# Spectral-filter weights: −k rows loaded from GpSimd's queue beside the +k rows from SyncE's, rows of 513 elements in place of 514

## The chip, the cores and the metric

The kernel runs on one core of one Trainium2 chip. The metric is the device time of one execution in microseconds (us). Engines are named as the profile names them: PE (TensorE, matmuls), PEld (its weight loads), DVE (VectorE), ACT (ScalarE), POOL (GpSimd), SP (SyncE, which only issues DMAs here); "SPq" is the issuing queue of SP.

## What is computed

Two spectral filters of the same input, mixed by a gate (B = 1, S = 2048, D = 1024, all bfloat16):

```python
def _ref(x, w_r, w_i):                       # once with A's weights, once with B's
    X = rfft2(x.astype(float32), axes=(-2, -1))
    X = X * (w_r + 1j * w_i)                 # w_r, w_i: [2048, 513]
    return irfft2(X, s=(S, D), axes=(-2, -1)).astype(bfloat16)

g = sigmoid((x * gate_w).sum(-1, keepdims=True))
out = g * A + (1 - g) * B
```

## The kernel before, in words

The Fourier transforms are matrix products with constant tables. The work runs in this order:

- **First stage** (L386 to L405): for each pair of row groups, DVE folds x (`fold`, L366, four TENSOR_TENSOR), PE multiplies by the table `FM` (eight matmuls for a group), ACT copies the result from PSUM to SBUF (tile `R3`). Along the way a gate row is made and summed (`gate_row`, L380; the matmuls of L413, which read the keys `zrow`).
- **Middle loop** (L538 on), t from 0 to 20. A pass issues, in this order: `stage_d(t)` (eight matmuls against `DM`, the result copied into the ring buffer, "RING"), `stage_s2(t-1)` (six matmuls against `S2`, the result X copied into `R4`), `stage_i1(0, t-5)` (eight matmuls against `KI`, the result V of filter A copied into `R1`), and in every second pass `prod(b, m)` (four DVE TENSOR_TENSOR: the complex product of X and the weights). At the end of pass 0 it calls `wload(1)`, then loads the tables `DI` and `RM`. The three matmul groups of a pass share three PSUM slots in turn (`slot`, L287), so a slot is free again when the copy of the group three before it has been made.
- **Then** `stage_i1(1, t)` with `stage_dinv(0, t)` (inverse transform of A) and the gate mix, and at last `stage_dinv(1, t)`, the final mix and the stores.

`ev` (L296) picks ACT or DVE for a copy out of PSUM by adding up estimated costs; the change alters none of them. Each engine executes its instructions in the order in which the program adds them.

The **weights** lie in SBUF as 128 partitions of 32 rows of `NS` = 514 elements: tile `R5` for filter A (b = 0), tile `R2` for filter B (b = 1). Partition 8j + 4·pm + ii holds 16 frequencies: pm = 0 is the +k rows, pm = 1 the −k rows, read with a negative step. One DMA of `wload` (L340) fills 16 partitions, those of one (pm, ii) with j = 0 to 15, with 16 rows each, of the real (c = 0) or the imaginary (c = 1) part. Tile `R2` is used before that for the gate row; tile `R1` holds x first, and V of filter A later. The profile calls `R1` to `R5` all "R".

The **order of engines and queues** is made by a small scheduler from keys that each operation reads and writes (L137):

```python
for k in reads:
    o.deps |= self.writer[k]
...
for k in writes:
    o.deps |= self.writer.get(k, set())
    o.deps |= self.readers.get(k, set())
for k in reads:
    self.readers.setdefault(k, set()).add(o)
for k in writes:
    self.writer[k] = {o}
    self.readers[k] = set()
```

So an operation that writes a key waits for the key's last writer and for all that have read it since. The DMAs of one `dma(...)` call (L318) are one operation with one semaphore, and a wait for it (L199) is a wait until all of its DMAs have landed; the wait stands in the waiting engine's queue ahead of the instruction. `allx` (L418) is the list of the keys ("x", 0) to ("x", 15); the first copy of V of filter A, in `stage_i1(0, 0)`, writes all of them (L482), since V takes the place of x. `wload(1)` writes ("W", 1) and the keys "zrow" and "gwt" (L362), since it takes the place of the gate row.

Of the kernel before, what the change touches and what calls it, by code (L numbers as in the profile page):

```python
# [7 lines left out]
AP = bass.AP  # L8
BF = dt.bfloat16

NS = 514
# [223 lines left out]
def bass_gated_mix__spectral_gfnet__spectral_gfnet__prompt_kernel(  # L235
# [6 lines left out]
    def sb(name, n, dty=BF):  # L242
        t = nc.alloc_sbuf_tensor(name, [128, n], dty)
        pit[id(t)] = n
        return t

    def ap(t, off, dims, p0=0, np_=128):
        return AP(t, p0 * pit[id(t)] + off, [[pit[id(t)], np_]] + [list(d) for d in dims])
# [18 lines left out]
    X5 = sb("X5", 32)  # L267
# [19 lines left out]
    def slot():  # L287
        s = slot_n[0] % nslots[0]
        slot_n[0] += 1
        return s  # L290

    def dve(ns, fns, reads, writes):
        load["dve"] += ns
        return S.op("dve", fns, reads, writes)

    def ev(n, outap, inap, reads, writes, eng=None, bias=0.0):  # L296
        ca, cd = 170 + 0.833 * n, 150 + 1.04 * n
        if eng is None:
            eng = "act" if load["act"] + ca <= load["dve"] + cd + bias else "dve"
        load[eng] += ca if eng == "act" else cd  # L300
        if eng == "act":
            S.op("act", lambda e: e.activation(outap, inap, ACT.Copy), reads, writes)  # L302
        else:
            S.op("dve", lambda e: e.tensor_copy(outap, inap), reads, writes)  # L304

    def pslot(s, off, dims, p0=0, np_=128):
        return ap(PS, s * 1024 + off, dims, p0, np_)
# [4 lines left out]
    def mm(o, l, r, start, stop):  # L312
        return lambda e: e.matmul(o, l, r, start=start, stop=stop, skip_group_check=True)  # L313

    def tt(o, a, b, op):
        return lambda e: e.tensor_tensor(out=o, in0=a, in1=b, op=op)  # L316

    def dma(eng, pairs, reads, writes, kind=True):  # L318
        S.op(eng, [lambda e, d=d, s=s: e.dma_start(d, s) for d, s in pairs], reads, writes, dma=kind)  # L319
# [19 lines left out]

    def wload(b):  # L340

        prs = []
        T = WR[b]
        P = pit[id(T)]
        for ii in range(4):
            for c in range(2):
                for pm in range(2):
                    src = wsrc[b][c]
                    n = src.shape[-1]

                    def part(r0, step, k0, k1, m=n + 1):
                        prs.append((AP(T, (4 * pm + ii) * P + (2 * k0 + c) * NS, [[8 * P, 16], [2 * NS, k1 - k0], [1, m]]),
                                    AP(src.tensor, src.offset + r0 * n, [[128 * n, 16], [step * n, k1 - k0], [1, m]])))
                    if pm == 0:
                        part(16 * ii, 1, 0, 16)
                    elif ii < 3:
                        part(80 + 16 * ii, -1, 0, 16)
                    else:
                        part(127, -1, 1, 2, n)
                        part(126, -1, 2, 16)  # L360
                        part(64, 1, 0, 1)
        dma("sp", prs, [], [("W", b)] + (["zrow", "gwt"] if b else []))  # L362
    wload(0)


# [44 lines left out]
    for n2 in range(16):  # L410
        w = ap(R2, n2 * 128, [[1, 128]], 0, 1)
# [6 lines left out]
    allx = [("x", m) for m in range(16)]  # L418
# [34 lines left out]
    def prod(b, m):  # L453

        T = WR[b]
        x = ap(R4, 2 * m * 1024, [[1024, 2], [512, 2], [1, 512]])
        w = ap(T, 2 * m * 2 * NS, [[2 * NS, 2], [NS, 2], [1, 512]])
        ws = ap(T, 2 * m * 2 * NS + NS, [[2 * NS, 2], [-NS, 2], [1, 512]])
        r = [("X", 2 * m), ("X", 2 * m + 1), ("W", b)]
        p = PO + m % 2 * 2048  # L460
        dve(1230, tt(ap(RING, TO, [[1024, 2], [512, 2], [1, 512]]), x, w, ALU.mult), r, ["t0"])
        dve(1230, tt(ap(RING, TO + 2048, [[1024, 2], [512, 2], [1, 512]]), x, ws, ALU.mult), r, ["t1"])
        for c, op in enumerate((ALU.subtract, ALU.add)):
            t = TO + 2048 * c
            dve(680, tt(ap(RING, p + c * 512, [[1024, 2], [1, 512]]), ap(RING, t, [[1024, 2], [1, 512]]),
                        ap(RING, t + 512, [[1024, 2], [1, 512]]), op), [f"t{c}"], [("P", m % 2, c)])
# [3 lines left out]
    def stage_i1(b, kg):  # L470
        s = slot()
        p = PO + kg // 2 % 2 * 2048 + kg % 2 * 1024
        z = 512 if kg == 0 else 0
        fns = []
        for lb in range(4):
            for c in range(2):
                w = ap(RING, p + c * 512 + lb % 2 * 256 + lb // 2, [[2, 128]])
                fns.append(mm(pslot(s, lb * 256, [[1, 256]]), w, ap(KI, z + c * 256, [[1, 256]]), c == 0, c == 1))
        S.op("pe", fns, [("P", kg // 2 % 2, 0), ("P", kg // 2 % 2, 1), "KI"], [("ps", s)])
        w = [("V", b, kg)]  # L480
        if kg == 0:
            w += allx if b == 0 else [("W", 0)]  # L482
        ev(1024, ap(VR[b], kg * 8, [[128, 128], [1, 8]]), pslot(s, 0, [[8, 128], [1, 8]]), [("ps", s)], w)

    def x512():
# [2 lines left out]
    def p512(b):  # L488
        T, o = WR[b], b * 96
        x = ap(X5, 0, [[16, 2], [1, 16]])  # L490
        w = ap(T, 512, [[NS, 2], [2 * NS, 16]])
        ws = ap(T, NS + 512, [[-NS, 2], [2 * NS, 16]])
        r = ["X5", ("W", b)]
        dve(100, tt(ap(P5, o, [[16, 2], [1, 16]]), x, w, ALU.mult), r, [("p5", b, 0)])
        dve(100, tt(ap(P5, o + 32, [[16, 2], [1, 16]]), x, ws, ALU.mult), r, [("p5", b, 1)])
        for c, op in enumerate((ALU.subtract, ALU.add)):
            dve(100, tt(ap(P5, o + 64 + 16 * c, [[1, 16]]), ap(P5, o + 32 * c, [[1, 16]]),
                        ap(P5, o + 32 * c + 16, [[1, 16]]), op), [("p5", b, c)], [("P5", b, c)])
# [39 lines left out]
    for t in range(16 + 5):  # L538
        if t < 16:
            stage_d(t)  # L540
        if 1 <= t < 17:
            stage_s2(t - 1)
        if t >= 5:
            stage_i1(0, t - 5)
        if t >= 2 and t % 2 == 0:
            prod(t // 18, t // 2 - 1 - t // 18 * 8)
        if t == 0:
            wload(1)
            cload("sp", DI, "DI", 2048)
            cload("sp", RM, "RM", 2048)  # L550
        if t == 17:
            x512()
            p512(0)
            p512(1)
        if t == 19:
            v512(0)
            v512(1)
# [14 lines left out]
    for t in range(16 + LAG):  # L572
        if t < 16:
            stage_i1(1, t)
            if t % 2 == 1 and t // 2 + 2 < 8:
                prod(1, t // 2 + 2)
        if t in (8, 10, 12, 14):
            gmix((t - 8) // 2)
        if t == 15:
            v512_row(1)  # L580
        if t >= LAG:
            stage_dinv(0, t - LAG)
# [64 lines left out]
```

## Time and profile before

| | |
|---|---|
| median of 2 runs | 159.06 us (158.91 to 159.21) |
| the profiled execution, its own time | 158.91 us |
| its span in the profile | 157.1 us |
| busy time: PE / ACT / DVE / POOL | 125.9 / 121.8 / 120.4 / 0.2 us |
| loaded from HBM / stored | 15.18 / 4.19 MB |
| mean granted TensorE clock | 0.962 |

The span runs from the first to the last instruction of the program; 1.8 us of the execution's own time lie outside it. The page cuts the span into 40 slices of 3.93 us and gives in tenths how busy each engine was. A line such as "A <- B: 8.4, 5, 6.4" in the view of the waits says that A waited for B 8.4 us in total, five times, at most 6.4 us. In the timeline, each row has the start, the length, the engine, the line of the code, and out<-in; "x2" says that two instructions were merged into the row.

### The profile page before, as it was taken

Reading aid. Unit: us, or ns where it says so; the run is one execution under the profiler, and the core shown is the slowest. Engines: PE = TensorE matmul, PEld = TensorE weight load, DVE = VectorE, ACT = ScalarE, POOL = GpSimd, SP = SyncE. Lnnn points to the kernel's source line nnn. Section 1 sums busy time; section 2 is a strip of 40 time slices with the busy share of each in tenths; the row PEclk is TensorE's granted clock in tenths of the full one; section 3 lists DMA queues with packets and bytes.
Section 4 is the critical chain, followed back from the end, with each engine's and each line's share of the span. In section 5 each row is a group of like instructions: output and inputs, shape, how many; then the busy total and the mean of one; then the engine's idle time right before and its main releaser. Section 6 shows DMA issues by size and latency. Waiting matters only on the chain.

```text
span 157.1 us, 2545 instructions
## 1 busy us (share of the span) xinstructions
PE 125.9 (80%) x1015; PEld 90.5 (58%) x1024; DVE 120.4 (77%) x193; ACT 121.8 (78%) x132; POOL 0.2 (0%) x4
## 2 busy tenths in 40 slices
PE   0145887788989999999657999959999899898930
PEld 0144653445665777776434688947778576565600
DVE  0689999000589898989999999949923788989893
ACT  3045789719999899799934699999998599888860
POOL 0000000000000000000000000000000000000000
PEclk9999999999999999999975599999999999999997
DMA  5999999999999970000000000000000033243433
GB/s 147 321 417 425 288 232 229 238 220 215 220 224 223 225 259 0 0 4 0 0 0 0 1 4 0 0 0 4 0 0 1 4 121 146 86 183 112 160 129 140
DMA packets 13230, 19.55 MB, mean 124 GB/s; under 512 B 1569, under 2 KB 9889, under 8 KB 12834
## 3 DMA queue, kind: packets, MB, share of 16 engines
q1 hardware_dynamic: 13072, 19.39, 45.2%
q8 instruction: 8, 0.13, 0.4%
q14 instruction: 4, 0.03, 0.1%
q10 hardware_dynamic: 146, 0.00, 0.1%
HBM read 15.18 MB, written 4.19 MB: 123 GB/s over the span
## 4 chain that ended last, share of the span: by engine, by line
PE 37%; ACT 30%; DVE 21%; issue 6%; DMA 4%; SPq 1%; DVEq 0%
PE PS L313 37%; ACT RING L302 14%; ACT R L302 13%; DVE RING L316 11%; DVE R L316 6%; DMA R<-in_A_x_dram 4%; DVE RING L304 3%; ACT GROW L565 1%; ACT V L302 1%; SPq L319 1%; DVEq L213 0%
## 5 line engine op out<-in xcount | busy, mean ns | idle before, releaser
L302 ACT ACTIVATE R<-PS 128x1024 bf16<-128x1024 f32 (+1 forms) x80 | 76.0, 1038 | 19.1 <-PE PS L313 19.0
L316 DVE TENSOR_TENSOR RING<-R 128x2048 bf16<-128x2048 bf16 (+1 forms) x48 | 48.0, 1041 | 14.1 <-ACT R L302 8.4
L302 ACT ACTIVATE RING<-PS 128x1024 bf16<-128x1024 f32 x40 | 42.9, 1138 | 8.0 <-PE PS L313 6.8
L316 DVE TENSOR_TENSOR RING<-RING 128x512 bf16<-128x512 bf16 (+1 forms) x96 | 44.6, 509 | 2.7 <-ACT RING L302 1.4
L313 PE MATMUL PS<-KI,RING 128*128 128x256 bf16 x256 | 35.4, 289 | 4.3 <-DVE RING L316 2.2
L313 PE MATMUL PS<-DI,R 128*128 128x256 bf16 x256 | 32.7, 273 | 1.5 <-DVE RING L304 1.2
L313 PEld LDWEIGHTS PS<-KI,RING 128*128 128x128 bf16 x256 | 25.0, 103 | 11.2 <-ACT R L302 2.9
L313 PEld LDWEIGHTS PS<-DI,R 128*128 128x128 bf16 x256 | 24.4, 98 | 8.4 <-DVE RING L304 2.2
L313 PE MATMUL PS<-FM,R 128*128 128x128 bf16 x128 | 11.6, 263 | 13.3 <-DVE R L316 13.3
L313 PEld LDWEIGHTS PS<-FM,R 128*128 128x128 bf16 x128 | 9.9, 120 | 15.1 <-DVE R L316 14.7
L313 PE MATMUL PS<-RING,S 128*128 128x1 bf16 (+2 forms) x91 | 15.8, 304 | 1.3 <-ACT RING L302 1.1
L313 PE MATMUL PS<-DM,R 128*128 128x256 bf16 x128 | 16.5, 273 | 0.3 <-ACT RING L302 0.2
L313 PEld LDWEIGHTS PS<-DM,R 128*128 128x128 bf16 x128 | 11.8, 98 | 3.0 <-ACT RING L302 1.1
L313 PEld LDWEIGHTS PS<-RING,S 128*128 128x128 bf16 x96 | 7.8, 97 | 7.5 <-ACT RING L302 1.4
L304 DVE CAST RING<-PS 128x1024 bf16<-128x1024 f32 x8 | 10.0, 1250 | 1.7 <-PE PS L313 1.7
L316 DVE TENSOR_TENSOR R<-RING 128x1024 bf16<-128x1024 bf16 x16 | 10.4, 688 | 0.3
L313 PE MATMUL PS<-R,FM 128*128 128x512 bf16 x30 | 9.1, 379 | 1.3 <-DVE RING L304 1.3
L313 PE MATMUL PS<-RING,DM 128*128 128x512 bf16 x30 | 9.1, 379 | 0.1
L313 PE MATMUL PS<-R,G 128*1 128x512 bf16 x32 | 7.5, 378 | 0.7 <-ACT R L302 0.7
L304 DVE CAST R<-PS 128x1024 bf16<-128x1024 f32 x4 | 4.9, 1222 | 3.1 <-PE PS L313 3.1
L316 DVE TENSOR_TENSOR FM<-RM,GROW 128x512 bf16<-128x512 bf16 x4 | 1.7, 422 | 5.4 <-ACT GROW L565 5.4
L316 DVE TENSOR_TENSOR ZG<-PS,GS 128x16 bf16<-128x16 f32 x1 | 0.2, 175 | 6.8 <-PE PS L313 6.8
(25 smaller groups left out, 28.7 us busy)
## 6 DMA issues: line engine op xcount, KB each, us to landing
out_dram<-RING SPq DMA_DIRECT2D x16, 256.0 KB, 2.0
R<-in_A_x_dram SPq DMA_DIRECT2D x3, 1024.0 KB, 10.6
R<-in_A_w_r_dram SPq DMA_DIRECT2D x7, 257.0 KB, 10.4
R<-in_A_w_i_dram SPq DMA_DIRECT2D x7, 257.0 KB, 10.3
R<-in_B_w_r_dram SPq DMA_DIRECT2D x7, 257.0 KB, 7.1
R<-in_B_w_i_dram SPq DMA_DIRECT2D x7, 257.0 KB, 8.1
R<-in_A_x_dram SPq DMA_DIRECT2D x2, 512.0 KB, 5.2
FM<-c_F SPq DMA_DIRECT2D x1, 512.0 KB, 5.2
```

The source lines that it names most:

```text
L302: S.op("act", lambda e: e.activation(outap, inap, ACT.Copy), reads, writes)
L304: S.op("dve", lambda e: e.tensor_copy(outap, inap), reads, writes)
L313: return lambda e: e.matmul(o, l, r, start=start, stop=stop, skip_group_check=True)
L316: return lambda e: e.tensor_tensor(out=o, in0=a, in1=b, op=op)
L319: S.op(eng, [lambda e, d=d, s=s: e.dma_start(d, s) for d, s in pairs], reads, writes, dma=kind)
L565: S.op("act", lambda e: e.activation(ap(GROW, 0, [[1, 512]]), misc(7, 0, [[1, 512]]), ACT.Sigmoid), ["m7"], ["GROW"])
```

## The change

`wload` collects the DMAs of the two signs in two lists. The +k list goes out from SP as before; the −k list goes out from POOL, as an operation that also reads the key ("x", 15). The keys become ("W", b, 0) and ("W", b, 1), and both operations of `wload(1)` write "zrow" and "gwt". Each row is read as 513 elements; before, all but two DMAs of a call read 514 (the padding column of the tile took the extra one). With that, the two DMAs for the first 15 rows of the last −k block become one. A call makes 8 DMAs on SP and 10 on POOL; before it was 20 on SP. The readers of the weights wait for both keys.

```diff
     def wload(b):
 
-        prs = []
+        both = ([], [])
         T = WR[b]
         P = pit[id(T)]
...
                 for pm in range(2):
                     src = wsrc[b][c]
                     n = src.shape[-1]
-
-                    def part(r0, step, k0, k1, m=n + 1):
-                        prs.append((AP(T, (4 * pm + ii) * P + (2 * k0 + c) * NS, [[8 * P, 16], [2 * NS, k1 - k0], [1, m]]),
-                                    AP(src.tensor, src.offset + r0 * n, [[128 * n, 16], [step * n, k1 - k0], [1, m]])))
+                    prs = both[pm]
+
+                    def part(r0, step, k0, k1):
+                        prs.append((AP(T, (4 * pm + ii) * P + (2 * k0 + c) * NS, [[8 * P, 16], [2 * NS, k1 - k0], [1, n]]),
+                                    AP(src.tensor, src.offset + r0 * n, [[128 * n, 16], [step * n, k1 - k0], [1, n]])))
                     if pm == 0:
                         part(16 * ii, 1, 0, 16)
                     elif ii < 3:
                         part(80 + 16 * ii, -1, 0, 16)
                     else:
-                        part(127, -1, 1, 2, n)
-                        part(126, -1, 2, 16)
+                        part(127, -1, 1, 16)
                         part(64, 1, 0, 1)
-        dma("sp", prs, [], [("W", b)] + (["zrow", "gwt"] if b else []))
+        dma("sp", both[0], [], [("W", b, 0)] + (["zrow", "gwt"] if b else []))
+        dma("pool", both[1], [("x", 15)], [("W", b, 1)] + (["zrow", "gwt"] if b else []))
     wload(0)
...
-        r = [("X", 2 * m), ("X", 2 * m + 1), ("W", b)]
+        r = [("X", 2 * m), ("X", 2 * m + 1), ("W", b, 0), ("W", b, 1)]
...
         if kg == 0:
-            w += allx if b == 0 else [("W", 0)]
+            w += allx if b == 0 else [("W", 0, 0), ("W", 0, 1)]
...
-        r = ["X5", ("W", b)]
+        r = ["X5", ("W", b, 0), ("W", b, 1)]
```

## The prediction

> **What bounds the kernel now.** I read the 40 slices first, for the stretch in which weights move, then the waits, the timeline around the first use of filter A's weights, and the chain of work at that place.
>
> ```profile
> PE   0145887788989999999657999959999899898930
> DVE  0689999000589898989999999949923788989893
> ACT  3045789719999899799934699999998599888860
> PEclk9999999999999999999975599999999999999997
> DMA  5999999999999970000000000000000033243433
> GB/s 147 321 417 425 288 232 229 238 220 215 220 224 223 225 259 0 0 4 0 0 0 0 1 4 0 0 0 4 0 0 1 4 121 146 86 183 112 160 129 140
> ```
>
> The DMA engines are busy without a break for 15 slices (to 59 us). x and tables move at 417 to 425 GB/s, the weights at 215 to 238, half of that. But does anybody wait for them?
>
> ```profile
> DVE RING L316 <- ACT R L302: 8.4, 5, 6.4
> DVE RING L316 <- DMA R<-in_A_x_dram: 5.7, 2, 4.4
> SPq L319 <- PE PS L313: 4.4, 1, 4.4
> ```
>
> (The third line is from SP's own list of waits.) In the whole list, x is the only load that an engine waits for. The first product (DVE RING L316) waits 6.4 us for X, copied by ACT, and not for the weights. By the trace's landings filter A's last weight DMA lands at 37.6 us (issued 29.3, 8.3 later) and filter B's at 57.3; their first readers start at 40.9 and after 76. So faster weights have nothing to shorten: gain 0. Only a loss is possible, where a wait moves. The place that matters is the middle loop:
>
> ```profile
> 34.32 1.23 SPq L319 DMA_DIRECT2D R<-in_B_w_r_dram  x2
> ...
> 40.91 2.36 DVE L316 TENSOR_TENSOR RING<-R 128x2048 bf16<-128x2048 bf16 x2 [6.41 <-ACT R L302]
> ...
> 45.16 1.03 PE L313 MATMUL PS<-KI,RING 128*128 128x256 bf16 x8
> ...
> 46.05 2.00 ACT L302 ACTIVATE R<-PS 128x1024 bf16<-128x1024 f32 x2
> ...
> 47.20 1.06 PE L313 MATMUL PS<-RING,S 128*128 128x512 bf16 x6
> ...
> 47.84 1.42 ACT L302 ACTIVATE RING<-PS 128x1024 bf16<-128x1024 f32 x1
> ```
>
> 34.32 is when SP is released to load filter B's weights (the PE wait of 4.4 us above: the matmuls that read "zrow"). 45.16 is `stage_i1(0, 0)`; of the two ACT copies at 46.05 the second is its V. The chain has them too:
>
> ```profile
> 46.26 1.79 ACT R L302 x2
> 48.05 1.22 ACT RING L302
> 49.27 0.05 issue
> 49.32 3.71 PE PS L313 x30
> ```
>
> So V(0,0) holds ACT from about 47.15 to 48.05, on the path that sets the end; then comes the copy of `stage_d(6)`, and PE runs from there almost without a gap (11.89 us of the 12 from 60 to 72).
>
> [...] 232 GB/s from 18 to 34 us, 221 from 38 to 54. [...] SP's unhindered weight DMAs (34.3 to 40 us) take 0.61 us each, [...] no run here shows GpSimd's. [...] from 76.80 to 80.21 PE was busy 1.47 of 3.41 us, and from 80.21 to 90.45 the clock was 0.50[...].
>
> **The change part by part.**
>
> *Rows of 513.* 64 of the 8192 rows were 1026 bytes already; their packet records take 86 ns on average, those of 1028 bytes 79. They sit in one-row DMAs beside semaphore writes, so from 0 to +9% on a row. I take 0; +9% would add 0.9 us to the +k half of filter B.
>
> *Filter A's weights.* SP's eight DMAs follow the tables as before. POOL (busy 0.2 us in all) starts when the last x load lands, 15.7 us (issued 3.1, 12.6 later). [...] Cost 0, hidden by ACT's X chain. Without that cover, every us past 40.9 would delay the first product, and it is reached only if POOL needs over 24 us.
>
> *Extra semaphore waits* at DVE and ACT: the issue gaps in the chain are 0.02 to 0.06 us, so under 0.2 in all; taken as 0.
>
> *The key ("x", 15).* It is meant to start POOL late, but it also makes both POOL operations readers of x. `stage_i1(0, 0)` writes all keys of x, and `wload(1)` was added before it, in pass 0. So the copy V(0,0) now waits until filter B's −k weights have landed. Before, these had until 76 us. Behind that wait in ACT's queue stand the copy of `stage_d(6)` and all later ones; PE can still do `stage_d(6)` and `stage_s2(5)` (to 48.3), then it has no free slot. DVE can do one copy and two products ahead, which are not on the path.
>
> *The keys "zrow" and "gwt".* Both operations of `wload(1)` write them, so the second, POOL's, waits for the landing of the first, SP's. The halves of filter B come one after the other, not beside each other.
>
> When does V(0,0) start, then? SP released 34.3. Eight DMAs of 16 x 16 x 1026 B = 0.263 MB at 221 GB/s: 9.5 us. Issue and landing: a store of 256 KB lands after 2.0 us, of which 0.6 is data at 425 GB/s, so 1.4. +k landed: 34.3 + 1.4 + 9.5 = 45.2. [...] the last, small DMA lands 1.2 later (R<-V of 4 KB: 1.7 from issue, 0.57 of it issuing): 61.3. Stall: 61.3 - 47.15 = 14.2 us, and nothing hides it, since PE, DVE and ACT all run dry. DI and RM, behind SP's half, move meanwhile; needed past 90.
>
> *PE clock.* PE idles from 48.3 to about 62.3, [...] PE is the bound there, [...] I take 2.5 (0 if the clock isn't cut).
>
> Sum: 14.2 + 2.5 = 16.7. Profiled execution: span 157.1 to 173.8, its time 158.9 to 175.6; against the median of 159.06, 0.15 above it, 175.8, said as **176 us**.
>
> Both ends of POOL's price: if it writes as fast as SP issues (6.1 us for ten), the transfer binds: 45.2 + 1.4 + 9.5 = 56.1, stall 9.0, time 168 without and 170.6 with the slow clock. Above, 2.5 us for each DMA, four times SP's 0.61 (an estimate): 25 us, V at 71.4, stall 24.2, time 186.
>
> **Rivals.**
>
> 1. *The transfer binds* (writing takes under 11.5 us): 168 to 172. [...]
> 2. *POOL is slow* (over 19 us for ten DMAs): 180 to 187. For it: nothing in this trace bounds it from above.
> 3. *Not slower:* POOL's second operation is not held by SP's. It then starts at 34.3, [...] and with ten DMAs in less than 47.15 - 34.3 - 1.2 = 11.6 us V(0,0) is not late: 159. It decides at 1.16 us for each DMA. Against: the rule on writers in the scheduler; it needs my reading of the keys to be wrong.
> 4. *Faster,* [...] no engine waits for weights, so this has next to no room.
>
> **How the numbers follow.** Chances: forecast (172 to 180) 0.59, rival 1 0.17, rival 2 0.17, rival 3 0.05, rival 4 0.02. What can be told from no change is about 2% (3.2 us): slower 0.93, within 0.05, faster 0.02. The range 168 to 186 takes in the ends of rival 1 and most of rival 2, and leaves out rivals 3 and 4. The forecast's own range is 172 to 180.
>
> **What would show it.** In the profile after: ACT R L302 idle some 14 us before V(0,0), ended by a DMA issued by POOL; a hole in PE, DVE and ACT from about 48 to 61 us, and a clock of 0.5 in the slices just after it; POOL's first filter B DMA just after the +k half has landed (about 45); the later stages as long as before. Wrong, if POOL's filter B DMAs start near 34, if V(0,0) starts on time, or if the hole lies at 40.9 (filter A late).

## The result, and the profile after

The changed kernel takes 181.97 us (median of 2 runs, 180.98 to 182.96) against 159.06: a ratio of 1.144, interval 1.117 to 1.171. A later set with 6 runs (below) gave 1.144 again, 1.139 to 1.149. The forecast was 176, in a range of 168 to 186. The profiled execution took 182.96 us with a span of 181.1: 24.0 us more than before. It is the slower of the two runs.

The 40 slices of the page (now 4.53 us each) have the hole:

```profile
PE   0445998889600004999999559999699989998950
DVE  0799990008950000268998999998693469899994
ACT  2255498399400005689889844899999959987970
PEclk9999999999975555599999985999999999999997
DMA  6999999999998990000000000000000003334334
GB/s 180 331 423 374 171 224 222 218 165 166 166 243 169 161 144 0 0 5 2 0 0 4 0 0 0 5 0 0 4 0 0 1 4 116 116 138 157 121 114 171
```

Slices 12 to 15 are empty on PE and ACT (DVE still has one copy and two products in slices 11 and 12), the clock is cut from within the hole to the first slices after it, and the weights move at 144 to 169 GB/s where one queue works alone (slices 9 to 11 and 13 to 15). The view of the waits names the two waits of the forecast:

```profile
POOL R L319 <- DMA R<-in_B_w_i_dram: 32.5, 1, 32.5
ACT R L302 <- DMA R<-in_B_w_i_dram: 22.0, 1, 22.0
POOL R L319 <- DMA R<-in_A_x_dram: 15.4, 1, 15.4
DVE RING L316 <- DMA R<-in_A_w_i_dram: 6.8, 1, 6.8
```

POOL waits for filter B's +k half, ACT for its −k half. The last line is new as well: the first product now waits for filter A's weights, but they come only 0.4 us after X, which it waited for before (41.36 against 40.94, the end of X's copy); when the same kernel ran again (e9), they came in time. The timeline around the hole:

```profile
46.09 1.10 ACT L302 ACTIVATE R<-PS 128x1024 bf16<-128x1024 f32 x1
46.38 1.05 PE L313 MATMUL PS<-DM,R 128*128 128x256 bf16 x8
47.26 1.06 PE L313 MATMUL PS<-RING,S 128*128 128x512 bf16 x6
...
53.93 0.58 POOL L319 DMA_DIRECT2D R<-in_B_w_r_dram  x1 [32.47 <-DMA R<-in_B_w_i_dram]
...
69.20 1.02 ACT L302 ACTIVATE R<-PS 128x1024 bf16<-128x1024 f32 x1 [22.01 <-DMA R<-in_B_w_i_dram]
70.12 1.31 ACT L302 ACTIVATE RING<-PS 128x1024 bf16<-128x1024 f32 x1
...
70.28 1.89 PE L313 MATMUL PS<-KI,RING 128*128 128x256 bf16 x8 [21.96 <-ACT R L302]
```

69.20 is V(0,0). PE did `stage_d(6)` and `stage_s2(5)` and then stood still for 22 us; the first eight matmuls after the hole take 1.89 us where such a group took 1.03. The chain of work runs through the two halves one after the other:

```profile
38.94 14.71 DMA R<-in_B_w_i_dram
53.65 0.28 issue
53.93 4.41 POOL R L319 x8
58.34 0.57 POOLq L213
58.91 10.21 DMA R<-in_B_w_i_dram
69.11 0.02 issue
```

### The profile page after: what moved, and what is told of

It is laid out like the page before. It is cut to its first block, busy times and chain, and to the rows that moved or that the text cites. A ratio compares the mean times of both kernels' runs of the same rounds, so it can differ in the third digit from the quotient of the medians.

```text
span 181.1 us, 2542 instructions
## 1 busy us (share of the span) xinstructions
PE 129.4 (71%) x1015; PEld 91.9 (51%) x1024; DVE 120.6 (67%) x193; ACT 121.6 (67%) x132; POOL 11.3 (6%) x24
## 4 chain that ended last, share of the span: by engine, by line
ACT 31%; PE 27%; DMA 17%; DVE 13%; issue 5%; SPq 3%; POOL 2%; POOLq 0%; DVEq 0%; ACTq 0%
PE PS L313 27%; ACT R L302 20%; DMA R<-in_B_w_i_dram 14%; ACT RING L302 8%; DVE RING L316 7%; DMA R<-in_A_x_dram 4%; DVE R L316 3%; SPq L319 3%; DVE RING L304 3%; POOL R L319 2%; ACT GROW L566 1%; ACT L566 1%; ACT V L302 1%; POOLq L213 0%; DVEq L213 0%
## 5 line engine op out<-in xcount | busy, mean ns | idle before, releaser
L316 DVE TENSOR_TENSOR RING<-R 128x2048 bf16<-128x2048 bf16 (+1 forms) x48 | 48.0, 1041 | 14.2 <-DMA R<-in_A_w_i_dram 6.8
L313 PE MATMUL PS<-KI,RING 128*128 128x256 bf16 x256 | 35.9, 291 | 26.4 <-ACT R L302 24.1
L313 PE MATMUL PS<-RING,S 128*128 128x1 bf16 (+2 forms) x91 | 16.7, 315 | 1.3 <-ACT RING L302 0.8
L313 PE MATMUL PS<-DM,R 128*128 128x256 bf16 x128 | 17.3, 282 | 0.1
L313 PEld LDWEIGHTS PS<-DM,R 128*128 128x128 bf16 x128 | 12.4, 101 | 2.9 <-ACT RING L302 0.7
L313 PE MATMUL PS<-R,G 128*1 128x512 bf16 x32 | 8.8, 423 | 0.7 <-ACT R L302 0.7
L313 PEld LDWEIGHTS PS<-R,G 128*1 128x1 bf16 x32 | 2.6, 90 | 5.8 <-issue 2.0
L313 PEld LDWEIGHTS PS<-RING,DM 128*128 128x128 bf16 x32 | 3.1, 98 | 3.8
```

## The experiments

My theory: the whole loss is V(0,0) waiting for filter B's −k half, plus a slow PE clock after the hole. The rivals: POOL's DMAs, or the slower loads, cost something by themselves; the serial halves cost by themselves. A second question came from the result: why the weights move at 165 GB/s and not at 221.

**Both waits taken away** (e4_keys_apart). The last x load and the gate row's readers write keys of their own for POOL's sake (only the ends of the long lines are shown):

```diff
-[], [("x", i) for i in range(a, b)])
+[], [("x", i) for i in range(a, b)] + (["xl"] if b == 16 else []))
...
-"ONE"], ["m7", "gwt"])
+"ONE"], ["m7", "gwt", "gwt1"])
...
-["ONE"], ["m7", "zrow"])
+["ONE"], ["m7", "zrow", "zrow1"])
...
-dma("pool", both[1], [("x", 15)], [("W", b, 1)] + (["zrow", "gwt"] if b else []))
+dma("pool", both[1], ["xl"], [("W", b, 1)] + (["zrow1", "gwt1"] if b else []))
```

> The changed kernel without its two waits: the last x load writes a key of its own that POOL reads in place of (x, 15), so that V(0,0) no longer waits for filter B; and POOL's half of filter B has keys of its own for the gate row, so that it no longer waits for SP's half. My theory (the loss is the wait of V(0,0), and the slow clock that follows it): 159 to 160, the 0.45 us by which filter A is late at the first product at most. Rival (POOL's DMAs disturb the engines by themselves, or the slower loads do): 165 or more.

Measured: ratio 0.998 (0.995 to 1.000). All 23 us are gone, with the weights on the same queues and in the same short rows. POOL's queue and the rate cost nothing by themselves.

**The x wait alone taken away** (e5_xkey_apart): only the two lines with "xl".

> The changed kernel with only the x wait taken away (POOL reads a key of its own in place of (x, 15)); POOL's half of filter B still waits for SP's. My theory: the half lands at 69 as before, but its first reader is the product of filter B after 76, so nothing waits: 159 to 160. Rival (the serial halves cost by themselves): over 165.

Measured: 1.0015 (0.9986 to 1.0044). POOL's half still starts late, and the view of the waits still shows its wait; but nobody waits for that half any more:

```profile
POOL R L319 <- DMA R<-in_B_w_i_dram: 31.6, 1, 31.6
```

So a half that lands at 68.7 us is harmless; the key ("x", 15) is what makes it cost.

**The gate-row wait alone taken away** (e6_rowkey_apart): only "zrow1" and "gwt1".

> The changed kernel with only the wait of POOL's half on SP's half taken away (keys of its own for the gate row); V(0,0) still waits for POOL's half. The two signs then run side by side from 34.4, and POOL's queue got 165 to 180 GB/s beside SP in filter A: 2.1 MB after filter A's rest, landing at about 50 to 53. V(0,0) is then late by 3 to 6 us, with the slow clock 5 to 9 in all: 163 to 168. If the serial halves were no part of the loss: 180.

Measured: 1.058 (1.054 to 1.063), 9.2 us slower. In its timeline V(0,0) starts at 54.75:

```profile
54.75 1.02 ACT L302 ACTIVATE R<-PS 128x1024 bf16<-128x1024 f32 x1 [7.90 <-DMA R<-in_B_w_i_dram]
```

So the serial halves are worth the rest, some 14 of the 23 us, but only through the wait of V(0,0). The half landed at 54.7, later than the 50 to 53 expected; filter A's weights drained until 40.5.

**The x wait alone put into the kernel before** (e7_before_xkey), for filter B, all from SP:

```diff
-        dma("sp", prs, [], [("W", b)] + (["zrow", "gwt"] if b else []))
+        dma("sp", prs, [("x", 15)] if b else [], [("W", b)] + (["zrow", "gwt"] if b else []))
```

> The kernel before with one wait added: the call for filter B (from SP, both signs) also reads (x, 15), so that V(0,0) waits for all of filter B, which lands at 57.3. My theory: stall 57.3 - 47.15 = 10.1 us and 2 to 3 of slow clock: 171 to 172. Without a clock loss: 169. Rival (the wait isn't the cause): 159.

Measured: 1.070 (1.067 to 1.073), 11.0 us slower, at a stall of 9.4 us. One key, without POOL, makes the loss:

```profile
56.70 1.03 ACT R L302
57.73 0.05 issue
57.78 8.28 PE PS L313 x49
```

This is its chain of work from V(0,0) on (the view ends at 66 us); just ahead of it stands the landing of filter B's last DMA at 56.61. The time, 169.2 us, is the one expected without a clock loss, but by chance: the stall was shorter than expected, and the kernel before took 158.2 us in this set; 1.6 us are left over beside the stall.

**Rows of 514 again, else as changed** (e1_rows514), the old `part` with `m=n + 1` and the split of the last block:

> The changed kernel with rows of 514 elements again (two −k DMAs split as before), all else as changed. Theory L (row length: rows of 1026 bytes are slow, 1.62 us for a DMA of 16 x 16 rows, and 1028-byte rows would take 1.19): filter B's +k half lands at about 47.5, the −k half at about 59, V(0,0) starts there, stall 12 us, time about 173. Theory P ([...] a stream of one sign alone is slow, whatever the row length): the 256 KB DMAs stay at about 1.6 us, V(0,0) at 69, time 181 to 183.

Measured: 1.107 (1.102 to 1.112), 17.0 us slower. The stall is 16.0 us, V(0,0) at 63.06. It lies between the two theories: the short rows make 6 of the 22 us of stall, but with rows of 514 filter B still doesn't move at 221 GB/s: from 48.4 us to the landing at 62.97 it is 183 on average (128 GB/s over the 20.8 us to 69.2, the tables behind the +k half in it), against 168 in the changed kernel from 48.4 us to 69.12.

**The kernel before with rows of 513** (e2_before_rows513), with the last −k DMAs joined as in the changed kernel, and **with all +k DMAs of a call first** (e3_before_by_sign), collected in two lists as there:

```diff
-                    def part(r0, step, k0, k1, m=n + 1):
+                    def part(r0, step, k0, k1, m=n):
```

```diff
-        dma("sp", prs, [], [("W", b)] + (["zrow", "gwt"] if b else []))
+        dma("sp", both[0] + both[1], [], [("W", b)] + (["zrow", "gwt"] if b else []))
```

> The kernel before with rows of 513 elements, both signs in turn from SP. Theory L: the weights move at about 162 GB/s, filter A's last lands at about 45, so the first product starts some 4 us late: 163 to 164. Theory P: 215 to 235 GB/s as before, same time, 159.

> The kernel before (rows of 514, all from SP) with all +k DMAs of a call ahead of its −k DMAs. Theory P: 162 to 170 GB/s, filter A's last lands at about 44 to 45, first product some 4 us late, 163 to 164. Theory L: about 221 GB/s, same time, 159.

Measured: 1.001 (0.999 to 1.004) and 1.000 (0.997 to 1.002). In e3 the first product starts 0.8 us late, at 41.74, and the time is the same. Neither property alone gives the slow rate (table below), so neither theory was right by itself.

**Both together, all from SP** (e12_rows513_by_sign):

> The kernel before, all from SP, with both properties of the changed stream: rows of 513 and all +k DMAs of a call ahead of the -k ones. If the two together make the slow rate, whatever the queue: 160 to 170 GB/s, filter A's last load lands at about 44 and the first product starts 3 us late, which the wait for X had covered until 40.9. If the loop has that much room behind it: same time; if the first product sets the end: 162. If the rate comes from POOL's queue beside SP's: about 190 GB/s as with either property alone.

Measured: 1.015 (1.009 to 1.021), 2.4 us slower; its runs spread more than the others', from 160.2 to 164.7 us. In the profiled one (162.5) the first product starts at 45.07, 4.2 us later than before, and nearly all of that reaches the end (span 161.0 against 157.1), with a clock cut of 3.4 us at 48.7 in it. The rates, from the view by stretch (24 to 32 us, while filter A is loaded), side by side:

| queue and order | rows of 514 | rows of 513 |
|---|---|---|
| SP, both signs in turn | 233 (before; 222 from 50 to 54 us) | 233 (e2; 208 from 50 to 54 us) |
| SP, one sign at a time | 195 (e3) | 170 (e12) |
| SP one sign, POOL the other, at once | 257 (e1) | 223 (changed) |

```profile
24.00:32.00 8.00, 7.08 (x61) 3.61 (x59) 3.31 (x6) 7.00 (x9) 0.00 (x0) 1.00 1.14 170
```

This row is e12's; the last number is GB/s, the one before it the share of the DMA engines. They are as busy at 170 GB/s as in the kernel before at 233 (1.13), with 1389 packets in these 8 us against 1921: in this stream each row takes longer. So the slow rate is made by the short row and by one sign at a time together, and not by POOL's queue.

**Rows of 514 without both waits** (e8_keys_apart_514):

> The changed kernel without both waits and with rows of 514. Nothing waits for weights, so the same as before whatever theory of the rate holds: 158.5 to 159.5; filter A no longer late at the first product if row length is the cause of the slow rate.

Measured: 1.002 (0.999 to 1.005). Filter A lands at 38.3, in time. No version beats the kernel before: none makes anything earlier that is waited for.

**The slow clock** (e9, e10, e11). The changed kernel again (e9), and matmuls that nobody reads in the hole, so that PE doesn't idle: 92 in the changed kernel (e10), 36 in that of e7 (e11):

```diff
+        if t == 6:
+            S.op("pe", [mm(misc(7, 0, [[1, 512]]), ap(KI, 0, [[1, 128]]), ap(DM, 0, [[1, 512]]), True, True)
+                        for _ in range(92)], ["KI", "DM"], ["m7"])
         if t >= 5:
             stage_i1(0, t - 5)
```

> The changed kernel itself once more, with more repetitions, to fix the size of the loss beside the next two. Stall of V(0,0) 22 us and 1 to 2.5 us of slow clock: ratio to the kernel before about 1.145 to 1.155.

> The changed kernel with 92 matmuls of 512 columns added on PE ahead of stage_i1(0, 1), some 20 us of work that fits into the hole of 22 us (their result is overwritten unread). If the slow clock after the hole is what comes on top of the stall: PE keeps its full clock and the time falls by 1 to 2.5 us against the changed kernel, leaving the stall alone. If the excess has another cause: the same time or longer.

> The kernel before with the added x wait (stall 9.4 us, 11.0 us slower), and 36 such matmuls (7.7 us) in its hole of 9.35 us. Clock theory: slower than before by the stall alone, 9.4 us, about 1.6 less than without them. Otherwise 11 us as without.

Measured: e9 1.144 (1.139 to 1.149), stall 21.1 us; e10 1.137 (1.132 to 1.143), 1.1 us less, but the intervals overlap; e11 1.078 (1.074 to 1.083), slower than e7 and not faster. The times alone decide nothing. The traces say why. In e11 filter B landed at 58.4 and not at 56.6, so the stall grew to 11.1 us, and the added matmuls ended 3.3 us too early: PE idled again, and the clock was cut anyway, but for 3.4 us in place of 10.2. In e10's profiled execution, the longest of its runs, the half landed late too (stall 23.9 us), PE idled for 3.4 us, and the clock was cut for 3.4. Counted from V(0,0) to the end of the span, e11 takes 110.3 us (168.8 − 58.5), e7 110.9 (167.6 − 56.7).

What the times could not show, the stretches of the traces can, set beside each other. The stall is from the profile's wait of ACT, the loss is the ratio less 1 times the median of the kernel before in the same set (158.2 to 158.3 us). "Loop" is the time from the end of V(0,0) to the start of the copy of `stage_d(15)`, less the 23.79 us that it takes in the kernel before; "half clock" is how much of it ran at a granted clock of 0.5:

| | stall of V(0,0), us | slower, us | rest | half clock, us | loop, us longer |
|---|---|---|---|---|---|
| e6 | 7.9 | 9.2 | 1.3 | 2.8 | 0.95 |
| e7 | 9.4 | 11.0 | 1.6 | 4.7 | 1.9 |
| e11 | 11.1 | 12.4 | 1.3 | 3.2 | 1.15 |
| e1 | 16.0 | 17.0 | 1.0 | 5.0 | 2.0 |
| e9 (changed) | 21.1 | 22.8 | 1.7 | 4.6 | 1.9 |
| changed, first profile | 22.0 | | | 6.1 | 2.6 |

The rest doesn't grow with the stall: 1.0 to 1.7 us once there is a hole, known to no better than the loss is, 0.5 to 0.8 us either way. The last two columns are finer. In e4, e5 and e8, which have no hole, the loop takes 23.78 to 23.80 us, as before. After a hole it is longer, and by more the longer the clock was at half, not the longer the stall was. The code of e7 and e11 differs by the added matmuls alone; these are their lines for the copy of `stage_d(15)` in e7, and for V(0,0) and that copy in e11:

```profile
83.40 1.34 ACT RING L302
58.51 1.03 ACT R L302
84.48 1.33 ACT RING L302
```

From the end of V(0,0), e7 needs 25.67 us and e11 24.94: the matmuls took 1.5 us from the half clock and 0.7 us from the loop, though the stall had grown by 1.7 us. So the slow clock is what comes on top of the stall. In the changed kernel the granted clock (third number from the end: 0.60, 0.50, 1.00) is half until 76.3:

```profile
48.40:69.20 20.80, 0.00 (x0) 0.00 (x0) 3.80 (x4) 0.00 (x0) 5.49 (x10) 0.60 0.91 167
69.20:76.30 7.10, 6.02 (x27) 3.69 (x28) 1.29 (x2) 5.21 (x5) 0.00 (x0) 0.50 0.00 0
76.30:84.00 7.70, 7.65 (x64) 5.77 (x64) 5.55 (x6) 6.35 (x7) 0.00 (x0) 1.00 0.02 4
```

## Why the prediction was right

The mechanism was right: who waits for what, and which two keys make the wait. The size was hit in part by luck. 182 us lies in the stated range of 168 to 186, but not in the forecast's own of 172 to 180; it lies in the band of rival 2, "POOL is slow", and POOL was fast (0.56 us for each DMA). Several terms of the sum were mis-sized, not all in one direction.

*Nothing to gain.* Right: e4, e5 and e8 move the weights in other ways and take the same time.

*The key ("x", 15).* Right, and shown both ways: taking it out of the changed kernel (e5) removes the whole loss, putting it alone into the kernel before (e7) makes 11.0 us.

*The keys "zrow" and "gwt".* Right: POOL started 0.28 us after the +k half had landed; without them (e6) the loss is 9.2 instead of 22.8 us. Rival 3, which needed this wait to be absent, would have been slower even so: V(0,0) was 7.9 us late, for POOL's half took until 54.7, although POOL's 0.56 us for each DMA met that rival's condition of 1.16.

*POOL's price* was mis-sized: between the +k half's landing at 45.2 and the last landing at 61.3 the forecast has 14.9 us for ten DMAs, the author's estimate, which no run had shown; measured 5.6 and 5.5 us.

```profile
L319 POOL DMA_DIRECT2D R<-in_B_w_r_dram x5 | 2.8, 557 | 32.5 <-DMA R<-in_B_w_i_dram 32.5
L319 POOL DMA_DIRECT2D R<-in_B_w_i_dram x5 | 2.8, 555 | 0.0
```

0.56 us for each DMA, small ones too, and less than SP's 0.61 (median for filter B, before and after). The first packet of POOL's half of filter B started at 55.20, 1.27 us after POOL began its first DMA; ten DMAs at 0.56 us did not pay that ten times. A busy DVE didn't hold POOL up here: it was busy for 5.50 of the first 5.60 us and for none of the second 5.49, at the same pace. By itself this error would have been rival 1, "the transfer binds", at 168 to 172.

*The rate* was mis-sized the other way: eight DMAs of one sign in 9.5 us, at 221 GB/s. That rate belongs to both signs in turn; the half took 12.4 us once filter A had drained (41.24 to 53.65). The stream in which the forecast read 232 and 221 GB/s alternated between the signs, and so was no measure of one; a stream of one sign in long rows moved at 195 (e3). The −k half took 15.2 us from POOL's first DMA (53.93) to the landing (69.12), where I had 16.1: here the two errors cancel.

*The start of the +k half* lacked a term. Filter B's DMAs queue behind filter A's, which had landed at 37.6 in the kernel before, a number that the forecast had read and not used here. Now filter A landed at 41.2, and the +k half at 53.65 and not at 45.2: 1.9 us late because the queue was not empty (37.6 in place of 34.3 + 1.4), 3.6 because filter A drained later, 2.9 by the rate. With 0.6 us back in the −k half, this is what the forecast lacks: the stall is 22.0 us and not 14.2.

*Short rows at 0 to +9% a row, taken as 0:* wrong in size, and the largest part of the difference. In the kernel before the 64 short rows sat among long ones. In a stream of one sign they cost 13% (195 to 170 GB/s), and with rows of 514 in the same queues (e1) filter A landed at 38.0 and the stall was 16.0 us: they make 6 of the 7.8 us by which the stall exceeds the forecast, spread over the two terms above.

*The clock:* forecast 2.5 us, the author's estimate; 1.0 to 1.7 in the timed sets. In the profiled execution V(0,0) ends 22.2 us later than before (70.23 against 48.05 in the chains), and the copy of `stage_d(15)`, some 26 us on, starts 24.7 us later (96.57 against 71.84). So 2.5 us were lost at half clock. Of that 0.7 came back by the end, where the later cut of the clock, near the loop's end, lasted 6.8 us and not 10.2; e4, which has no hole and a later cut of 6.8 us, is 0.8 us shorter there. What sets the granted clock the traces don't show: in the kernel before it fell to 0.50 at 80.21, and PE had not been idle in the 3.41 us ahead of it but busy for 1.47; in e6 the full clock came back at 58.53, when PE had been busy for 2.71 of the 3.41 us before, while in the kernel before 3.06 of 3.42 us busy (83.62 to 87.04) did not bring it back. That stays open.

Sum as measured in that execution: 22.2 + 2.5 - 0.7 = 24.0 us, where I had 14.2 + 2.5 = 16.7.

What stays open: why a row of 1026 bytes is slower than one of 1028. The loss is 13% with one sign at a time (195 to 170 GB/s) or both at once (257 to 223), and between nothing (24 to 32 us, 233 in both) and 6% (50 to 54 us, 222 to 208) with both in turn. Why one sign at a time is slower than both in turn (195 against 233 GB/s in rows of 514) was not shown either.

## What to carry to other kernels

When a load is split over two queues, read what the new operations' keys do to others: a key read "to start late" makes its operation a reader that every later writer of the key must wait for, and two operations that write one key run one after the other. A load that nobody waits for can only lose by being changed; ask first who will now wait for it. A rate measured on a mixed stream is not the rate of one part of it (here 233 GB/s for both signs in turn, 195 for one, both from 24 to 32 us).

## What the runs showed of the hardware

POOL's DMAs join rows: of its packets in the changed kernel from 24 to 32 us, 334 have 4104 bytes, four rows, where 389 of SP's have 1026, one row. With both queues full, the engines served as many packets of the one as of the other. From the DMA view of that stretch (packets, those of 4 bytes included, MB, share):

```profile
q0 software_dynamic: 416, 1.37, 77.3%
q1 hardware_dynamic: 417, 0.40, 28.0%
```

So POOL's queue (q0) gets 3.4 times SP's bytes.

The stretches of half clock around the holes lasted 3.41 us in e11, 6.83 in e6, 10.24 in e7, 17.07 in e1, 20.48 in e9 and 23.89 in the changed kernel's first profile: 1, 2, 3, 5, 6 and 7 times 3.41.

The same stream of filter B, from 48 to 54 us, moved at 236 GB/s in e7, when PE and ACT stood almost still, at 214 in e11, where only the added matmuls ran, and at 222 in the kernel before. One profile each; that busy engines slow the loads is not shown by more than that.
